# The attention output of blocks 2 to 14 turned by transposing transfers, and the first sums of the down weights later

## The chip, the cores and the metric

The kernel runs on one core of a Trainium2 chip. The metric is the device time of one execution in microseconds (us), the median of several runs. The profile names the engines PE (TensorE, matrix products; PEld loads the stationary operand), DVE (VectorE), ACT (ScalarE), POOL (GpSimd) and SP (SyncE, which here issues nearly all transfers).

## The reference

One transformer block on x of 2048 rows and 640 columns in float32: layer norm, attention of 32 heads of 20 columns in which a row sees itself and the 255 rows ahead of it, the product with wo added to x, and a gated feed-forward layer with 1536 hidden columns.

```
def _A_ref(x, wqkv, wo):          # H = 32, Dh = 20, W = 256
    q, k, v = ...                 # (x @ wqkv) by heads
    scores = einsum("bhqd,bhkd->bhqk", q, k) * Dh ** -0.5
    mask = (idx[:, None] - idx[None, :] >= 0) & (idx[:, None] - idx[None, :] < W)
    p = softmax(where(mask, scores, -1e9))
    o = einsum("bhqk,bhkd->bhqd", p, v)
    return o.transpose(0, 2, 1, 3).reshape(B, S, D) @ wo
def _B_ref(x, w_gate, w_up, w_down):
    return (gelu(x @ w_gate) * (x @ w_up)) @ w_down
h  = x + _A_ref(layernorm(x), wqkv, wo)
h2 = h + _B_ref(layernorm(h), w_gate, w_up, w_down)
```

## The kernel before, in words

**Tiling.** The 2048 rows are 16 blocks of 128 rows (j = 0 to 15). A dense product of float32 precision is made of three products of halves: each operand is split into a float16 "hi" (a cast) and a float16 "lo" (the value less hi), and hi·hi, hi·lo and lo·hi are summed in PSUM. `parts` (line 556) lists the three, `products` (568) issues them, and `quarters` (560) cuts a 128-wide stationary operand into four 32-wide ones where the planner takes PE to be in the state in which the p·v products leave it. PE contracts over partitions, so an operand whose columns are contracted must be turned first: 128 rows by 640 columns become five squares of 128 by 128.

**Stages.** In the first some 640 us attention and the first parts of the feed-forward layer run interleaved; behind that the feed-forward layer runs alone, with a scheme that saves products by sums of operands (`Quad`, `down7`). For a block of attention: x is loaded and normalised (`x_lane`, line 706), turned, multiplied into q and k, which go to DRAM and come back by heads (`stack`, line 801: six loads each into qT and kT on SP); maxima and scores are made for pairs of heads in PSUM (`ra`, `rb`), the exponentials by ACT (`pt`), the mask by POOL, p·v on PE (`pv`). ACT copies four steps of p·v into oT, and `normalise` (1081), once for each half of the heads, turns oT by four PE transposes into PSUM (`tp`), from which DVE takes the reciprocal of the row sums (`rec`) and writes the quotient into `o32` (printed `o` by the profile). Behind the second half `o_transpose` (1102) turns o32: five PE transposes in two groups (four and one) into PSUM, each followed by ACT's cast to oh and DVE's subtraction to ol (`transpose_part`, 543). Then the block's number goes into `woq`, and `wo_block` (1120) makes its products with wo (its halves are w3h and w3l); `wo_out` adds x on DVE and writes h on SP.

**Two ways to turn.** `transpose_part` is the one on PE. `turned` (526) is the other: ACT casts the whole block to hi, DVE subtracts to lo, both in an SBUF buffer that is read as two float16 halves, and SP issues a transposing transfer (DMA_TRANSPOSE) of 128 by 640 for each. x's blocks from 4 on use it, with the buffer `xp`, one copy of it, into xh and xl; h of the feed-forward layer uses it too. A counter lets one such turn of x begin at a time.

**What sets the order.** Each engine runs its instructions in the order in which the program issues them. That order is found when the program is built: the class Clock keeps an estimated clock for each engine, every piece of work is a generator (a "lane") that yields what its next instruction needs, and the loop at the end issues the next instruction of the first lane that could start, in a fixed order of lanes (work on finished PSUM results first, then turns, outputs, side work, then attention or dense products). `normalise` and `o_transpose` may be held back up to an estimated 2 us so that they fall between other kinds of products. SP's instructions stand in one order too; one that must wait for its data holds those behind it. All instructions are recorded by one helper, so all have line 199; the tiles tell them apart.

**Sums of down weights.** `seven_weights` (1398) prepares, for a later stage of the feed-forward layer, four sums of the halves of the down weights: POOL subtracts (ts<-w10l), DVE adds (ts<-w10h), POOL, DVE. Its first step waits in the planner until a count of finished "quads" has reached FT = 4 and two weights are used up.

Of the kernel before, what the change touches and what calls it, by code (L numbers as in the profile page):

```python
# [11 lines left out]
F32 = mybir.dt.float32  # L12
F16 = mybir.dt.float16
# [8 lines left out]
S, D, H, DH, F = 2048, 640, 32, 20, 1536  # L22
P = 128
NB = S // P
KC = D // P
# [5 lines left out]
FT = 4  # L31
# [18 lines left out]
def _pow2(e):  # L50
    return float(2.0 ** e)
# [202 lines left out]
def block_kernel(ctx: ExitStack, tc: tile.TileContext, x, wqkv, wo, wg, wu, wd, out):  # L254
# [12 lines left out]
    opened, pos = Counter(), Counter()  # L267
# [11 lines left out]
    def ps_tp(dt=F32):  # L279
        return bank("tp", dt)  # L280

    def done(name):
        opened[name] -= 1
# [10 lines left out]
    NR = 4  # L294
# [17 lines left out]
    def need(*reads, slots=(), when=None, eng="tensor"):  # L312

        def f():
            if when and not when() or any(opened[n] >= banks[n] for n in slots):
                return INF
            return max([nc.ready(reads, eng)]
                       + [nc.slot(psums[n], n, banks[n]) for n in slots])
        return f

    def pe(*reads, slots=(), when=None):
        return ("tensor",), need(*reads, slots=slots, when=when)

    def on(eng, *reads, when=None, after=None):
        f = need(*reads, when=when, eng=eng)
        if after is not None:
            return (eng,), lambda: max(f(), nc.others(after, eng))
        return (eng,), f
# [4 lines left out]
    def soon(eng, *reads):  # L333
        return Soon((eng,)), need(*reads, eng=eng)
# [143 lines left out]
    W = {}  # L478
# [47 lines left out]
    def turned(src, lane, to, dst=None, when=None, two=None):  # L526

        key = "xparts" if dst else "parts"
        yield on("scalar", src, when=lambda: not opened[key] and (not when or when()))
        opened[key] += 1  # L530
        two = (two if dst else lnbuf[2]).bitcast(F16)
        hi, lo = two[:, :D], two[:, D:]
        nc.scalar.copy(hi, src)
        yield on("vector", hi)
        nc.vector.tensor_tensor(lo, src, hi, op=ALU.subtract)
        if dst:
            to = dst()
        for o, i in zip(to, (hi, lo)):
            yield ("sync",), need(i, eng="sync")
            nc.sync.dma_start_transpose(o, i)  # L540
        opened[key] -= 1
# [99 lines left out]
    maxq, tps, scoreq, valq, woq = [], [], deque(), deque(), deque()  # L641
# [45 lines left out]
    class Block:  # L687
# [3 lines left out]
        h, turned, normed, full = None, False, False, False  # L691
# [7 lines left out]
    B = [Block() for _ in range(NB)]  # L699
# [3 lines left out]
        b.c, b.cols = C[j // 2], slice((j % 2) * P, (j % 2) * P + P)  # L703
    at = lambda n, shape, dt, bufs=2: nc.tile(att, shape, dt, n, bufs)

    def x_lane(blocks, lane):

        for j in blocks:
            c = C[j // 2]
            if j > 1:  # L710
                yield on("vector", when=lambda: W["k" if j < NR else "v"].scaled)
            if j >= NR and j + 1 < NB:
                yield ("sync",), lambda: max(0.0, nc.slot(att, "xt", 2))
                load_x(j + 1)

            def dst():
                if j < 2:
                    return x32[:, :, B[j].cols], None
                return xparts(j)

            yield from layernorm(B[j].x, lane, None, None, dst,
                                 lambda: j < 6 or c.x or C[j // 2 - 3].used == 4,
                                 lambda: B[j].x, tp="rb" if j in (1, 3) else "tp",
                                 dma=j >= NR and at("xp", [P, D], F32, 1))
            if j < 2:
                B[j].full = True
                tasks.append(x_cast(j))
            else:
                B[j].ready = True

    def xparts(j):
        c = C[j // 2]
        if c.x is None:
            c.x = tuple(nc.tile(wq, [P, KC, CW], F16, n, 3) for n in ("xh", "xl"))
        return tuple(t[:, :, B[j].cols] for t in c.x)

    def x_cast(j):
        src = x32[:, :, B[j].cols]
        yield on("scalar", src, when=lambda: W["k"].scaled)
        hi, lo = xparts(j)  # L740
        nc.scalar.copy(hi, src)
        yield on("gpsimd", hi)
        nc.gpsimd.tensor_tensor(lo, src, hi, op=ALU.subtract)
        B[j].ready = True

    def load_x(j):
        if 0 < j < NR:
            t = at("pt", [P, 4, 3, P], F32, 3).rearrange("p a b c -> p (a b c)")
            B[j].x = t[:, 0:D]
        else:  # L750
            B[j].x = at("xt", [P, D], F32)
        nc.sync.dma_start(B[j].x, x[j * P:(j + 1) * P, :])
# [328 lines left out]
    def normalise(j, half, oT):  # L1081
        b = B[j]
        yield pe(oT, slots=["tp"], when=lambda: j == 0 or half or B[j - 1].normal)
        if half == 0:
            b.o32 = at("o32", [P, H, DH], F32, 1)
        t = ps_tp()
        OR = 3 * 32 + DH + 1
        for u4 in range(4):
            nc.tensor.transpose(t[:, u4 * P:u4 * P + OR], oT[:OR, u4, :], ident[:OR, :OR])
        pos["normal"] += 1  # L1090
        tv = t.rearrange("p (h e) -> p h e", e=32)
        rec = at("rec", [P, 16], F32)
        yield soon("vector", t)
        nc.vector.reciprocal(rec, tv[:, :, DH])
        yield soon("vector", rec)
        nc.vector.tensor_tensor(b.o32[:, 16 * half:16 * half + 16, :], tv[:, :, 0:DH],
                                rec[:, :, None].to_broadcast([P, 16, DH]), op=ALU.mult)
        done("tp")
        if half:
            tps.append(o_transpose(j))  # L1100

    def o_transpose(j):
        b = B[j]
        src = b.o32.rearrange("p h d -> p (h d)")
        for part, (c0, c1) in enumerate(((0, 4), (4, 5))):
            yield pe(src[:, c0 * P:c1 * P], slots=["tp"],
                     when=lambda: part or j < 2 or B[j - 2].wrote)
            if part == 0:
                b.oh, b.ol = at("oh", [P, KC, P], F16), at("ol", [P, KC, P], F16)
            yield from transpose_part(src, b.oh, b.ol, c0, c1)  # L1110
        b.normal = True
        woq.append(j)
# [284 lines left out]

    def seven_weights():

        yield on("gpsimd", when=lambda: pos["quads"] >= FT and W["u", 1].spent  # L1400
                 and W["u", 2].spent)
        t = nc.tile(ffp, [P, KC, 512], F32, "ts0").rearrange("p c n -> p (c n)").bitcast(F16)
        n = FT * N2
        t1, t2, t3, t4 = ST["t"] = [t[:, i * n:(i + 1) * n].rearrange("p (f n) -> p f n", n=N2)
                                    for i in range(4)]
        ul = [W["u", g].hl[1].rearrange("p c f -> p (c f)") for g in (1, 2)]
        ST["z"] = [ul[0].bitcast(F32)[:, i * N2:(i + 1) * N2] for i in range(4)]
        ST["s"] = [ul[1][:, i * FT * P:(i + 1) * FT * P].rearrange("p (f n) -> p f n", n=P)
                   for i in range(4)]
        for g, (c, fg) in enumerate(SEVEN):  # L1410
            dh, dl = W["d", fg].hl
            d1, d2, e1, e2 = dl[:, :, :N2], dl[:, :, N2:], dh[:, :, :N2], dh[:, :, N2:]
            free = lambda n: lambda: pos["visits"] >= 8 * (g - 1) + n
            yield on("gpsimd", dl, when=free(6))
            nc.gpsimd.tensor_tensor(t1, d2, d1, op=ALU.subtract)
            yield on("vector", t1, dh, when=free(6))
            nc.vector.scalar_tensor_tensor(t2, e2, _pow2(-TE), t1, op0=ALU.mult, op1=ALU.subtract)
            pos["t", g] = 2
            yield on("gpsimd", t2, when=free(7))
            nc.gpsimd.tensor_tensor(t3, t2, d1, op=ALU.subtract)  # L1420
            pos["t", g] = 3
            yield on("vector", t2, when=free(8))
            nc.vector.scalar_tensor_tensor(t4, t2, -_pow2(TE), e1, op0=ALU.mult, op1=ALU.add)
            pos["t", g] = 4
# [457 lines left out]
    for i, n in enumerate("qkv"):  # L1882
        W[n].load(rooms[n])
        W[n].room(wq)
        if i:
            load_x(i + 1)
    load_x(NR)
    lanes = [x_lane([0], "x"), x_lane([1], "xb"), x_lane([2], "xc"), x_lane([3], "xd"),
             x_lane(range(NR, NB), "x"),
             split_lane(), *(scale_lane([i], str(i)) for i in range(NW)),  # L1890
             scale_lane(range(NW, len(weights)), "0"), load_lane(), ones_lane(), big_lane(),
# [95 lines left out]
```

## Time and profile before

| | before |
|---|---|
| median of 3 runs | 995.48 us (994.24 to 996.4) |
| profiled execution | 996.4 us |
| its span on the core | 994.7 us |
| granted PE clock, mean | 0.996 |
| DMA traffic | 113.01 MB, 114 GB/s in the mean |

The span is the time between the first and the last instruction on the core; 1.7 us of the profiled execution lie around it. An engine's busy time is the union of its instructions; PE's products overlap, so a group's duration is more than it holds PE. "x -> y" in the profile's rows is written y<-x: the tile written, then those read. A mark like [0.50 <-ACT oh] at a row's end is the idle time before it on its engine and what ended that.

### The profile page before, as it was taken

How to read it: one execution, taken by the hardware profiler on the slowest of the kernel's cores; microseconds unless marked ns; L12 is line 12 of the kernel's file. 1: busy time of each engine (PE TensorE's matmuls, PEld its weight loads, DVE VectorE, ACT ScalarE, POOL GpSimd, SP SyncE). 2: the span in 40 equal slices, each digit the busy share in tenths (PEclk: the TensorE clock that was granted, in tenths of full speed). 3: DMA queues.
4: the chain of work that ended last, by engine and by line, in shares of the span. 5: the costliest groups of instructions: out<-in, count | busy, mean ns of one | idle time of the engine just before them, and what ended most of it. 6: DMA issues, size and time to landing. Idle time of an engine off the chain costs nothing.

```text
span 994.7 us, 35811 instructions
## 1 busy us (share of the span) xinstructions
PE 977.8 (98%) x15326; PEld 747.6 (75%) x15326; DVE 787.4 (79%) x2252; ACT 485.7 (49%) x862; POOL 342.0 (34%) x498
## 2 busy tenths in 40 slices
PE   8998999999999999999999999999999999999998
PEld 7875777777877777777766754688788888888886
DVE  7878998887876767777688798877976887788784
ACT  5615657675555555555577535343323333443431
POOL 7003335463434333344346311344303223233320
PEclk9999999999999999999999999999999999999999
DMA  8667565752522433222305543324354442223211
GB/s 314 126 124 181 148 171 161 172 140 76 112 81 70 109 87 81 72 69 70 124 31 124 113 136 104 109 80 132 119 175 106 148 144 81 80 80 107 81 54 53
DMA packets 130047, 113.01 MB, mean 114 GB/s; under 512 B 85216, under 2 KB 103392, under 8 KB 129888
## 3 DMA queue, kind: packets, MB, share of 16 engines
q1 hardware_dynamic: 117792, 99.97, 36.6%
q10 hardware_dynamic: 12096, 10.75, 3.4%
q8 instruction: 120, 1.97, 0.8%
q14 instruction: 39, 0.32, 0.1%
HBM read 73.73 MB, written 28.84 MB: 103 GB/s over the span
## 4 chain that ended last, share of the span: by engine, by line
PE 86%; DVE 8%; ACT 3%; DMA 2%; issue 1%; POOL 0%; SPq 0%; ACTq 0%; DVEq 0%
PE mm L199 40%; PE rb L199 12%; PE ra L199 12%; PE pv L199 11%; PE tp L199 9%; DVE junk L199 1%; DVE ts L199 1%; DVE am L199 1%; ACT pt L199 1%; DVE ht L199 1%; DMA wst<-in_wu_dram 0%; DVE w1l L199 0%; DMA wst<-in_wd_dram 0%; DMA pt<-in_x_dram 0%; DVE xt L199 0%
## 5 line engine op out<-in xcount | busy, mean ns | idle before, releaser
L199 POOL TENSOR_SCALAR_AFFINE_SELECT pt<-pt 128x512 f32<-128x512 f32 x352 | 176.5, 517 | 270.0 <-ACT pt L199 252.6
L199 DVE CUSTOM_DVE_ANT_0 junk<-rb,band 128x320 bf16<-128x320 f32 x232 | 113.4, 489 | 36.1 <-PE rb L199 31.1
L199 ACT ACTIVATE pt<-ra,esc 128x640 f32<-128x640 f32 (+2 forms) x132 | 100.6, 769 | 78.0 <-PE ra L199 68.8
L199 ACT ACTIVATE pt<-rb,esc 128x640 f32<-128x640 f32 (+2 forms) x124 | 94.3, 768 | 81.9 <-PE rb L199 75.4
L199 DVE CUSTOM_DVE_ANT_0 junk<-ra,band 128x320 bf16<-128x320 f32 x216 | 105.7, 489 | 33.9 <-PE ra L199 28.9
L199 PE MATMUL pv<-pt,v 128*21 128x128 f32 x2880 | 103.0, 275 | 0.3 <-ACT oT L199 0.2
L199 PEld LDWEIGHTS <-ah 128*128 128x128 f16 (+1 forms) x660 | 63.5, 98 | 23.2 <-issue 1.0
L199 PEld LDWEIGHTS <-ws 128*128 128x128 f16 x720 | 70.8, 98 | 12.9 <-issue 2.6
L199 PEld LDWEIGHTS <-qT 60*64 60x64 f16 x1280 | 29.7, 104 | 62.3 <-issue 51.3
L199 PEld LDWEIGHTS pv<-pt,v 128*21 128x21 f32 x2880 | 69.2, 100 | 9.6 <-issue 1.1
L199 PEld LDWEIGHTS <-kT 62*64 62x64 f16 x2880 | 64.4, 106 | 9.3 <-issue 5.3
L199 PEld LDWEIGHTS <-gu 128*128 128x128 f16 (+1 forms) x700 | 51.7, 98 | 26.1 <-issue 0.4
L199 DVE SCALAR_TENSOR_TENSOR ht<-mm,ffk,ht 128x320 f32<-128x320 f32 x86 | 46.9, 545 | 15.4 <-PE mm L199 14.2
L199 PE MATMUL mm<-xh,w1h 128*32 128x256 f16 (+1 forms) x344 | 55.9, 273 | 1.4 <-DVE qks L199 1.4
L199 PE MATMUL mm<-xl,w1h 128*32 128x256 f16 (+1 forms) x362 | 56.0, 273 | 0.0
L199 PE MATMUL mm<-xh,w1l 128*32 128x256 f16 (+1 forms) x356 | 55.9, 273 | 0.0
L199 ACT CAST ah<-gel 128x512 f16<-128x512 f32 x48 | 29.7, 619 | 47.8 <-DVE gel L199 47.7
L199 DVE TENSOR_TENSOR al<-gel,ah 128x512 f16<-128x512 f32 x48 | 42.3, 882 | 13.1 <-ACT ah L199 12.1
L199 ACT ACTIVATE gel<-gel,ffk 128x512 f32<-128x512 f32 x36 | 26.0, 723 | 50.2 <-DVE gel L199 50.1
L199 PE MATMUL mm<-w3h,oh 128*32 128x320 f16 (+1 forms) x364 | 49.7, 299 | 0.6 <-DVE ht L199 0.6
L199 PE MATMUL mm<-w3h,ol 128*32 128x320 f16 (+1 forms) x355 | 49.6, 299 | 0.0
L199 PE MATMUL mm<-w3l,oh 128*32 128x320 f16 (+1 forms) x355 | 49.6, 299 | 0.0
(354 smaller groups left out, 2670.2 us busy)
## 6 DMA issues: line engine op xcount, KB each, us to landing
ws<-wsums SPq DMA_DIRECT2D x24, 640.0 KB
qk<-qks ACTq DMA_DIRECT2D x32, 256.0 KB
wsums<-ws SPq DMA_DIRECT2D x12, 640.0 KB
qT<-qk SPq DMA_DIRECT2D x72, 80.0 KB
kT<-qk SPq DMA_DIRECT2D x72, 80.0 KB
ht<-in_x_dram SPq DMA_DIRECT2D x16, 320.0 KB
h_dram<-ht SPq DMA_DIRECT2D x16, 320.0 KB
ht<-h_dram SPq DMA_DIRECT2D x16, 320.0 KB
```

Of the source, the lines that this page charges most:

```text
L199: r = real(*args, **kw)
```

## The change

Three edits. First, the buffer xp is taken once, ahead of `x_lane`, in place of a request in each block. Second, for blocks 2 to 14 `o_transpose` no longer turns o32 on PE: it calls `turned` with its own counter for o and x together, the same buffer xp, and fresh tiles oh and ol as the targets; it may begin once block j - 2 has written h. The block counts as normalised when its two transfers are issued, and the first half of `normalise` of the next block waits for that in the planner. Blocks 0, 1 and 15 are turned as before. Third, `seven_weights` begins at 2·FT = 8 finished quads in place of 4.

```
--- before.py
+++ after.py
@@ -703,6 +703,8 @@
+    xp = at("xp", [P, D], F32, 1)
+
     def x_lane(blocks, lane):
@@ -721,7 +723,7 @@
-                                 dma=j >= NR and at("xp", [P, D], F32, 1))
+                                 dma=j >= NR and xp)
@@ -1082,6 +1084,7 @@
         b = B[j]
         yield pe(oT, slots=["tp"], when=lambda: j == 0 or half or B[j - 1].normal)
         if half == 0:
+            yield pe(when=lambda: j == 0 or B[j - 1].normal)
             b.o32 = at("o32", [P, H, DH], F32, 1)
@@ -1102,6 +1105,15 @@
     def o_transpose(j):
         b = B[j]
         src = b.o32.rearrange("p h d -> p (h d)")
+        if 1 < j < NB - 1:
+            def dst():
+                b.oh, b.ol = at("oh", [P, KC, P], F16), at("ol", [P, KC, P], F16)
+                return b.oh, b.ol
+
+            yield from turned(src, "o", None, dst, lambda: B[j - 2].wrote, xp)
+            b.normal = True
+            woq.append(j)
+            return
         for part, (c0, c1) in enumerate(((0, 4), (4, 5))):
@@ -1397,7 +1409,7 @@
     def seven_weights():
 
-        yield on("gpsimd", when=lambda: pos["quads"] >= FT and W["u", 1].spent
+        yield on("gpsimd", when=lambda: pos["quads"] >= 2 * FT and W["u", 1].spent
                  and W["u", 2].spent)
```

The function it calls, as it stands in both:

```
def turned(src, lane, to, dst=None, when=None, two=None):
    key = "xparts" if dst else "parts"
    yield on("scalar", src, when=lambda: not opened[key] and (not when or when()))
    opened[key] += 1
    two = (two if dst else lnbuf[2]).bitcast(F16)
    hi, lo = two[:, :D], two[:, D:]
    nc.scalar.copy(hi, src)
    yield on("vector", hi)
    nc.vector.tensor_tensor(lo, src, hi, op=ALU.subtract)
    if dst:
        to = dst()
    for o, i in zip(to, (hi, lo)):
        yield ("sync",), need(i, eng="sync")
        nc.sync.dma_start_transpose(o, i)
    opened[key] -= 1
```

What the change moves, at three places. On PE at block 12, where the first four transposes of o32 stood between a score group (rb<-qT,kT) and dense products of v (w2h, w2l with x's halves):

```order
L199 LDWEIGHTS kT
L199 MATMUL rb<-qT,kT 64x64
L199 MATMUL tp<-ident,o_12167 128x128 x4
L199 LDWEIGHTS xl
L199 MATMUL mm<-w2h,xl 128x320
L199 LDWEIGHTS xh
L199 MATMUL mm<-w2h,xh 128x320
```

and where, in the changed kernel, the first product with wo now stands (w3h with oh), the rows around it:

```order
L199 LDWEIGHTS xh
L199 MATMUL mm<-w2l,xh 128x320
L199 LDWEIGHTS xl
L199 MATMUL mm<-w2h,xl 128x320
L199 LDWEIGHTS oh
L199 MATMUL mm<-w3h,oh 128x320
L199 LDWEIGHTS qT
L199 MATMUL rb<-kT,qT 64x320
```

The transposes are gone from between the scores; the first product with oh stands four pairs of maxima and scores behind the last transpose of oT, where it stood six behind it before, and one pair of maxima now separates it from the next product with wo.

On SP around block 8, before: the loads of q and k of one pair of blocks (six for each block), the write of h and the load of the next row of x for the residual.

```order
L199 DMA h_dram<-ht 128x640
L199 DMA ht<-in_x_dram 128x640
L199 DMA qT<-qk_8008 20x16x128 x6
L199 DMA kT<-qk_8793 20x16x128 x6
L199 DMA h_dram<-ht 128x640
```

And in the changed kernel, the same loads under other buffer numbers:

```order
L199 DMA h_dram<-ht 128x640
L199 DMA ht<-in_x_dram 128x640
L199 DMA qT<-qk_8266 20x16x128 x6
L199 DMA_TRANSPOSE oh<-xp 128x5x128
L199 DMA_TRANSPOSE ol<-xp 128x5x128
L199 DMA kT<-qk_8937 20x16x128 x6
L199 DMA h_dram<-ht 128x640
```

The two transposing transfers of o stand behind the six loads of qT and ahead of those of kT.

On DVE in the last stage, the first sums of the down weights (ts<-w10h) among the work on results of quads (gel, rs, ht) and on sums of h (wst), as a piece of the difference with its marks:

```order
 L199 TENSOR_TENSOR al<-gel,ah 128x512
 L199 SCALAR_TENSOR_TENSOR ht<-mm,ffk,ht 128x320
-L199 SCALAR_TENSOR_TENSOR ts_16367<-w10h,ts_16367 128x1280
-L199 TENSOR_TENSOR gel<-tp,rs 128x256
-L199 SCALAR_TENSOR_TENSOR ts_16367<-ts_16367,w10h 128x1280
+L199 TENSOR_TENSOR gel<-tp,rs 128x256
 L199 TENSOR_TENSOR rs<-rb,rs 128x256
 L199 TENSOR_TENSOR gel<-rb,gelt 128x256
```

The two sums come back some 27 rows later, on either side of a product's result (ht) and the product of gate and up (gel). POOL's rows keep their order there:

```order
L199 TENSOR_TENSOR ws<-w5h,ws 128x640
L199 TENSOR_TENSOR ts_16605<-w10l 128x1280
L199 TENSOR_TENSOR ts_16605<-ts_16605,w10l 128x1280
L199 TENSOR_TENSOR lyh<-lveh,mhalf 128x1
L199 TENSOR_TENSOR lyi<-lvei,mhalf 128x1
```

These five rows stand the same way in both kernels, under another buffer number.

## The prediction

> **What bounds the kernel now.** I read the page first, its totals and the chain that ended last:
>
> ```profile
> span 994.7 us, 35811 instructions
> PE 977.8 (98%) x15326; PEld 747.6 (75%) x15326; DVE 787.4 (79%) x2252; ACT 485.7 (49%) x862; POOL 342.0 (34%) x498
> PE 86%; DVE 8%; ACT 3%; DMA 2%; issue 1%; POOL 0%; SPq 0%; ACTq 0%; DVEq 0%
> PE mm L199 40%; PE rb L199 12%; PE ra L199 12%; PE pv L199 11%; PE tp L199 9%; DVE junk L199 1%; DVE ts L199 1%; DVE am L199 1%; ACT pt L199 1%; DVE ht L199 1%; DMA wst<-in_wu_dram 0%; DVE w1l L199 0%; DMA wst<-in_wd_dram 0%; DMA pt<-in_x_dram 0%; DVE xt L199 0%
> ```
>
> TensorE (PE) is busy for 98% of the span and holds 86% of the chain; ScalarE (ACT) is busy for half of it. A share over the whole span mixes stages, so I cut it. The columns are the window, its length, the busy time of PE, PEld, DVE, ACT and POOL with counts, the granted PE clock, the share of the DMA engines and their GB/s:
>
> ```profile
> 100.00:330.00 230.00, 227.45 (x5247) 175.08 (x5244) 191.99 (x702) 140.57 (x227) 101.68 (x181) 1.00 0.51 125
> 330.00:570.00 240.00, 239.55 (x5764) 175.61 (x5763) 178.75 (x606) 144.47 (x225) 100.16 (x197) 1.00 0.34 86
> 640.00:995.00 355.00, 348.71 (x2938) 288.14 (x2937) 276.53 (x515) 123.05 (x271) 98.79 (x63) 0.99 0.32 103
> ```
>
> The attention of blocks 2 to 14 lies in the first two windows. PE is idle there for 2.6 and 0.5 us, DVE for 38 and 61, ACT for 89 and 96. So a product taken from PE there shortens the run by what it took, as long as nothing arrives late in its place. The clock is at 1.00, so fewer products bring no faster ones.
>
> **What the first part removes.** The timeline of PE around block 12 shows the instructions that go, each row one group (start, length, tile written <- tiles read, count):
>
> ```profile
> 475.05 0.62 PE L199 MATMUL tp<-ident,oT 117*128 117x117 f32 x4
> 475.51 0.30 PE L199 MATMUL mm<-w2l,xh 128*128 128x320 f16 x1
> 478.56 0.66 PE L199 MATMUL tp<-ident,o 128*128 128x128 f32 x4
> 479.05 0.30 PE L199 MATMUL mm<-w2h,xl 128*128 128x320 f16 x1
> 482.36 0.33 PE L199 MATMUL tp<-ident,o 128*128 128x128 f32 x1
> 482.53 0.30 PE L199 MATMUL mm<-w2h,xl 128*128 128x320 f16 x1
> 486.39 0.30 PE L199 MATMUL mm<-w3h,oh 128*128 128x320 f16 x1
> ```
>
> Products are pipelined, so I price by the step from one start to the next: the four transposes hold PE for 479.05 - 478.56 = 0.49 us, the fifth for 482.53 - 482.36 = 0.17 us. That is 0.66 us a block, and for the 13 blocks 2 to 14 **8.6 us**. The groups of PE give the count and a second price:
>
> ```profile
> L199 PE MATMUL mm<-xh,w1h 128*128 128x256 f16 x152 | 41.5, 273 | 1.4 <-DVE qks L199 1.4
> L199 PE MATMUL tp<-ident,o 128*128 128x128 f32 x80 | 15.4, 290 | 0.0
> L199 PE MATMUL mm<-xh,w1h 128*32 128x256 f16 x192 | 14.4, 273 | 0.0
> ```
>
> 80 transposes are 16 blocks of five; 65 go. At 15.4 us busy for 80, 65 would be 12.5 us; those durations overlap, so it is the upper end and 8.6 the value.
>
> **What it adds on PE.** In the order of the changed kernel 44 more dense products stand in a place where they are cut into four 32-wide ones. Four such cost 14.4/48 = 0.300 us of busy time, one whole product 41.5/152 = 0.273: 27 ns each, 1.2 us for 44, the upper end, since the rows of both kinds overlap. I take it whole. Nine filling products fewer at the start bring nothing, because they stand where PE waits anyway. So PE's own work falls by 8.6 - 1.2 = **7.4 us**.
>
> **What it adds elsewhere.** DVE's, then ACT's part of the turn of block 12:
>
> ```profile
> 475.98 0.25 DVE L199 RECIPROCAL rec<-tp 128x16 f32<-128x16 f32 x1
> 476.27 0.49 DVE L199 TENSOR_TENSOR o<-tp,rec 128x320 f32<-128x320 f32 x1
> 480.07 0.69 DVE L199 TENSOR_TENSOR ol<-tp,oh 128x512 f16<-128x512 f32 x1 [0.50 <-ACT oh L199]
> 483.55 0.29 DVE L199 TENSOR_TENSOR ol<-tp,oh 128x128 f16<-128x128 f32 x1 [0.18 <-ACT oh L199]
> ```
>
> ```profile
> 479.46 0.58 ACT L199 CAST oh<-tp 128x512 f16<-128x512 f32 x1
> 483.26 0.26 ACT L199 CAST oh<-tp 128x128 f16<-128x128 f32 x1
> ```
>
> The same work for x's turn is in the view of the tile xp (shortest, median and longest ns):
>
> ```profile
> L199 ACT CAST xp<-xt x12: 710/725/736, 47.1 to 326.2; 128x640 f16<-128x640 f32 x12
> L199 DVE TENSOR_TENSOR xp<-xt,xp x12: 817/820/1247, 48.0 to 327.0; 128x640 f16<-128x640 f32 x12
> ```
>
> ACT goes from 0.58 + 0.26 = 0.84 to 0.73 us a block, DVE from 0.98 to 0.82 (1.25 at worst): a little less on two engines that have 39% (ACT) and 17% (DVE) or more to spare in those windows. That is worth nothing on the path. The price is latency: the halves must now be cast, subtracted and carried by two transfers before PE reads them. I bound it by x's own turns. The quickest one behind the first 100 us, and the slowest:
>
> ```profile
> 258.98 0.72 ACT L199 CAST xp<-xt 128x640 f16<-128x640 f32 x1
> 261.44 1.89 SPq L199 DMA_TRANSPOSE xl<-xp  x1
> ```
>
> ```profile
> 152.26 0.73 ACT L199 CAST xp<-xt 128x640 f16<-128x640 f32 x1
> 156.90 6.61 SPq L199 DMA_DIRECT2D kT<-qk  x3
> 164.95 1.21 SPq L199 DMA_TRANSPOSE xl<-xp  x1
> ```
>
> From the cast's start to the issue of the second transfer: 2.5 us, and 12.7 us where SyncE (SP) stood 6.6 us in loads of kT placed ahead of it. The landing shows where the first user waits for such a transfer, with h in the last stage:
>
> ```profile
> 758.65 1.82 SPq L199 DMA_TRANSPOSE h1h<-wsl  x1
> 761.70 0.73 ACT L199 CAST wsl<-wsl 128x640 f16<-128x640 f32 x1 [3.07 <-DMA h1h<-wsl]
> 761.42 1.20 SPq L199 DMA_TRANSPOSE h1l<-wsl  x1
> 764.09 0.82 DVE L199 TENSOR_TENSOR wsl<-wsl 128x640 f16<-128x640 f32 x1 [0.89 <-DMA h1l<-wsl]
> ```
>
> 761.70 - 758.65 = 3.05 us and 764.09 - 761.42 = 2.67 us from issue to landing. The chain of a block then is: from the last transpose of oT (about 475.4) to the end of o's second half (476.27 + 0.49) 1.35 us, cast to second issue 2.5, landing 2.7 to 3.05: 6.5 to 6.9 us, and with one ACT and one DVE instruction ahead about 8.2. I take **7.4**.
>
> What the chain has to fit into is the way on PE from the last transpose of oT to the first product with oh. Before, at block 12, it was 486.39 - 475.4 = 11.0 us with three rounds (a round is two pairs of maxima and scores, one step of p·v and the dense products between), 3.7 us a round. In the new order two rounds stand there, 7.3 us and a few dense products (7.9), and the product with ol one pair later. Blocks 2, 3 and 8 have two and a half rounds (9.0 to 9.4), the other nine 10.2 to 21.7; the 13 blocks average 12.1. So the undisturbed chain fits everywhere, barely at block 12, and a turn held like the slow one of x does not: 10.2 us later than the quick one, less 12.1 - 7.4 = 4.7 of room, is 5.5 us of PE standing still, and everything queued behind that product on PE (maxima, scores, p·v) stands with it. One in twelve of x's turns was held so; with 13 turns I expect one, and as much as none: the value is between 0 and 5.5, about **2.6 us**. The ends are 0 (no hold) and 17 (two holds at blocks with 9.2 us of room: 2 x (10.2 - 1.7)).
>
> SP itself issues 26 more transfers of about 1.2 us, 31 us in the 470 us of both windows; loads behind them come later by 2.4 us a block, and q and k rows are loaded well ahead of their use. Moving xp to one allocation for both users adds a wait only where x's turn and o's turn meet; they meet in blocks 2 to 8, and the key that lets one turn begin at a time puts o's behind x's by at most one quick turn, 2.5 + 2.7 us. The new wait in the first half's normalisation stands in the planner and not on the chip; it puts those transposes a little later in PE's order.
>
> The Trainium skill speaks against this edit: "VectorE: DVE Perf Modes", section "The three transpose paths" and the rules behind it, prices a 128x128 transpose at 390 ns on TensorE and 1309 ns by transfer, and keeps the transfer for destinations that can't be PSUM. By an estimate from that page a half of five squares would land after 6.5 us, both after 13.1, the chain would be some 15 us, and the run about 50 us longer; the landings above, 3.05 and 2.67 us for five squares, disagree, so I leave it no chance of its own.
>
> **The third part.** The later first sums of the down weights aim at a place where PE stands still:
>
> ```profile
> PE tp L199 <- ACT rr L199: 2.2, 1, 2.2
> ```
>
> ```profile
> 702.88 2.60 POOL L199 TENSOR_TENSOR ts<-w10l 128x1280 f16<-128x1280 f16 x1
> ```
>
> ```profile
> L199 DVE TENSOR_SCALAR wsl<-wsl,lmvi,lyi x6: 603/612/2853, 541.8 to 781.1; 128x640 f32<-128x640 f32 x6
> ```
>
> ```profile
> 702.97 2.85 DVE L199 TENSOR_SCALAR wsl<-wsl,lmvi,lyi 128x640 f32<-128x640 f32 x1
> ```
>
> DVE's instruction, 612 ns in the median of its six, starts 0.09 us after POOL's first sum and ends 0.3 us after it; what DVE and ACT have to do with PE's results comes late, and PE waits 2.2 us. But in POOL's new order that sum stands where it stood, behind the same sum of weights (ws<-w5h,ws) and with nothing of its own to wait for; only DVE's two sums (ts<-w10h) move, some 27 rows on. So the collision stays: **nothing**, with 2.2 us of gain (it goes) and 2.2 us of loss (a second one of its size) as ends. The Trainium skill, "SBUF — State Buffer", section "SBUF: two separate sides", calls the pair of ports that VectorE shares with GpSimd an exclusive lock, held for a whole instruction; the two rows agree, and by it the gap goes only if POOL's sum is moved.
>
> **The sum.** -7.4 + 2.6 + 0 = -4.8 us. The profiled run took 996.4 us, its span and 1.7 us around it; that is 0.9 above the median of 995.48. So 991.6 against the profiled run, **990.7** against the median. A measurement of this kernel can tell about 0.2%, 2 us, from no change.
>
> **Rivals.** *Given back*: one turn held fully at a block with little room (10.2 - 1.7 = 8.5 us) against 7.4 of gain: 996.6, or, with the average room of 4.7 us, 993.6. For it speaks that new transfers of blocks 4, 6 and 8 stand right behind six loads of qT, and those of 5, 7, 9 and 11 among loads of kT; against it that these loads mostly belong to a group that has begun. *Slower*: SP stands still in front of the transposing transfers at two of the blocks 2, 3, 8 and 12, because the loads ahead wait for rows of q and k that are not yet written. Price 2 x 8.5 = 17 us, less 7.4: 995.5 + 9.6 = 1005.1. It decides from 9.4 us of new waits on. *More gain*: no hold, the quarters at nothing and the collision gone: -8.6 - 2.2 = -10.8, 984.7; with the first two alone 986.9. That the first part doesn't do what it says is ruled out by the order; that the third doesn't is my forecast.
>
> **How the numbers follow.** Forecast (988 to 993.5) 0.62, more gain (below 988) 0.08, given back (993.5 to 997.5) 0.18, slower (above) 0.12. The range leaves out half of the gain's case, the upper end of the second and the slow case, about 0.2: 986.5 to 996.5. Faster by over 0.2% is the first two, 0.70; within 0.18; slower 0.12.
>
> **What would show it.** tp<-ident,o 15 times instead of 80, PE's busy time lower by 7 to 9 us; 13 transfers each into oh and ol; in the waits of PE a new line of dense products on the transfer of oh or ol, 0 to 6 us in all, at few blocks; the end of attention earlier by about what PE saved less that line; the 2.2 us on ACT rr still there. Wrong would be: waits on oh or ol above 7 us, a landing well over 3 us, or q and k loads that now arrive after PE asks for them.

## The result, and the profile after

| | before | after |
|---|---|---|
| median | 995.42 us (994.24 to 996.78, 6 runs) | 1006.41 us (1004.38 to 1011.55, 6 runs) |
| ratio to before | | 1.0122, 95% interval 1.0102 to 1.0141 |
| profiled execution, span | 996.4, 994.7 us | 1004.54, 1002.8 us |

The change makes the kernel 1.2% slower; the forecast was 0.5% faster. The page after, its totals and its chain:

```profile
span 1002.8 us, 35973 instructions
PE 974.0 (97%) x15384; PEld 741.3 (74%) x15384; DVE 788.2 (79%) x2239; ACT 486.2 (48%) x849; POOL 341.3 (34%) x498
PE 81%; DVE 10%; ACT 3%; issue 3%; DMA 1%; POOL 1%; ACTq 0%; SPq 0%; DVEq 0%; POOLq 0%
PE mm L199 40%; PE rb L199 11%; PE ra L199 11%; PE pv L199 11%; PE tp L199 8%; DVE junk L199 4%; ACT pt L199 1%; DVE ws L199 1%; DVE m L199 0%; DVE w1l L199 0%; ACTq L199 0%; DVE wsl L199 0%; DMA xh<-xp 0%; DMA ol<-xp 0%; DVE ht L199 0%
```

PE is busy for 3.8 us less (974.0 for 977.8), where the forecast had 7 to 9, and yet the span is 8.1 us longer. A part of the saving is hidden: the mean granted PE clock fell from 0.996 to 0.992, by estimate some 4 us of the span, and a product with oh lasts up to 474 ns, where its median is 299. PE's idle time, the span less its busy time, rose from 16.9 to 28.8 us. The windows (length, busy time of PE, PEld, DVE, ACT and POOL, granted PE clock, DMA share, GB/s) show where:

```profile
100.00:330.00 230.00, 218.48 (x5026) 165.21 (x5028) 183.19 (x662) 132.54 (x210) 94.30 (x170) 0.97 0.57 126
330.00:570.00 240.00, 238.21 (x5886) 172.54 (x5877) 182.87 (x621) 146.11 (x218) 105.33 (x205) 1.00 0.43 98
640.00:995.00 355.00, 351.69 (x2972) 290.54 (x2970) 285.19 (x526) 123.69 (x273) 98.61 (x64) 1.00 0.33 106
```

Between 100 and 330 us PE now stands idle for 11.5 us where it stood 2.6, and its clock is 0.97 in place of 1.00. What it waits for, by the list of PE's waits (sum, times, longest):

```profile
PE rb L199 <- ACT pt L199: 5.3, 2, 4.7
PE ra L199 <- DVE mxs L199: 4.4, 5, 2.1
PE tp L199 <- ACT rr L199: 2.7, 2, 2.2
PE ra L199 <- ACT pt L199: 2.6, 5, 0.7
PE pv L199 <- DVE pv L199: 2.5, 1, 2.5
```

The same list of before names no wait on ACT pt, and on DVE mxs these two lines:

```profile
PE ra L199 <- DVE mxs L199: 2.0, 1, 2.0
PE rb L199 <- DVE mxs L199: 1.1, 3, 0.6
```

So the waits that grew are on exponentials (ACT pt) and maxima (DVE mxs). A wait of PE for a transfer of oh or ol, which the forecast looked for, isn't among them.

The longest wait can be followed. PE first, then ACT, then SP around 151 us of the changed kernel (start, length; in brackets the idle time before and what ended it):

```profile
151.20 0.33 PE L199 MATMUL ra<-kT,qT 60*64 60x320 f16 x4
156.27 0.48 PE L199 MATMUL rb<-qT,kT 62*64 62x128 f16 x12 [4.75 <-ACT pt L199]
```

```profile
149.27 0.24 ACT L199 CAST h0h<-tp 128x128 f16<-128x128 f32 x1
154.80 0.72 ACT L199 CAST xp<-xt 128x640 f16<-128x640 f32 x1 [5.29 <-DMA xh<-xp]
155.43 0.79 ACT L199 ACTIVATE pt<-rb,esc 128x640 f32<-128x640 f32 x1
```

```profile
142.89 7.56 SPq L199 DMA_DIRECT2D kT<-qk  x6
150.55 1.24 SPq L199 DMA_TRANSPOSE xh<-xp  x1
151.90 2.30 SPq L199 DMA_TRANSPOSE xl<-xp  x1
```

SP stands in loads of kT for 7.6 us, so the transfer of xh is issued at 150.55, 12.3 us after its cast began at 138.23. ACT has come to the next block's cast into xp, which must not overwrite what that transfer still reads. It waits 5.29 us, and the exponential behind it, which waits for nothing of the kind, waits with it; so does PE. Both turns are of x: the first cast of o comes later, at 179 us. In the kernel before, the same turn (cast at 137.05) had its transfers ahead of most of these loads:

```profile
138.46 2.27 SPq L199 DMA_TRANSPOSE xh<-xp  x1
142.47 1.21 SPq L199 DMA_TRANSPOSE xl<-xp  x1
145.40 10.90 SPq L199 DMA_DIRECT2D kT<-qk  x7
```

### The profile page after: what moved, and what is told of

Same layout as the page of the kernel before. It is cut to its first block, busy times and chain, and to the rows that moved or that the text cites. A ratio compares the mean times of both kernels' runs of the same rounds, so it can differ in the third digit from the quotient of the medians.

```text
span 1002.8 us, 35973 instructions
## 1 busy us (share of the span) xinstructions
PE 974.0 (97%) x15384; PEld 741.3 (74%) x15384; DVE 788.2 (79%) x2239; ACT 486.2 (48%) x849; POOL 341.3 (34%) x498
## 4 chain that ended last, share of the span: by engine, by line
PE 81%; DVE 10%; ACT 3%; issue 3%; DMA 1%; POOL 1%; ACTq 0%; SPq 0%; DVEq 0%; POOLq 0%
PE mm L199 40%; PE rb L199 11%; PE ra L199 11%; PE pv L199 11%; PE tp L199 8%; DVE junk L199 4%; ACT pt L199 1%; DVE ws L199 1%; DVE m L199 0%; DVE w1l L199 0%; ACTq L199 0%; DVE wsl L199 0%; DMA xh<-xp 0%; DMA ol<-xp 0%; DVE ht L199 0%
## 5 line engine op out<-in xcount | busy, mean ns | idle before, releaser
L199 DVE CUSTOM_DVE_ANT_0 junk<-rb,band 128x320 bf16<-128x320 f32 x224 | 109.5, 489 | 35.9 <-PE rb L199 31.0
L199 DVE CUSTOM_DVE_ANT_0 junk<-ra,band 128x320 bf16<-128x320 f32 x224 | 109.5, 489 | 35.3 <-PE ra L199 30.3
L199 ACT ACTIVATE pt<-ra,esc 128x640 f32<-128x640 f32 (+2 forms) x131 | 98.1, 757 | 79.2 <-PE ra L199 68.1
L199 PEld LDWEIGHTS <-ah 128*128 128x128 f16 x648 | 63.4, 98 | 23.4 <-issue 1.1
L199 PE MATMUL mm<-xl,w1h 128*128 128x256 f16 (+1 forms) x344 | 56.1, 273 | 0.0
```

The source lines that it names most:

```text
L199: r = real(*args, **kw)
```

## The experiments

Two theories stood at the start. **A**: turns that meet in the one buffer xp make casts (ACT) and subtractions (DVE) stand, with exponentials and maxima behind them. **B**: the planner found another order, and the order of before is a good one among many.

To compare orders I priced PE's work from the traces: the median step between the starts of two products, for each pair of kinds in the trace of before, summed over a kernel's own order. What is left up to PE's last product is waiting and slower clock. A saving of work and a loss by waits are then told apart. The two columns are my estimate; no view of the profile has them, their level depends on how the kinds are drawn, and only their differences are used:

| run | ratio to before, 95% interval | PE work, us | rest, us |
|---|---|---|---|
| before | 1 | 962.4 | 25.9 |
| after | 1.0122 (1.0102 to 1.0141) | 954.6 | 41.5 |
| xp once | 1.0131 (1.0113 to 1.0148) | 962.3 | 37.4 |
| blocks 10 to 14 only | 1.0003 (0.9993 to 1.0014) | 959.8 | 27.1 |
| after, cast when xp is free | 1.0094 (1.0073 to 1.0115) | 955.1 | 41.3 |
| after, sums as before | 1.0105 (1.0079 to 1.0132) | 954.6 | 41.1 |
| xp once, marked | 1.0001 (0.9988 to 1.0013) | 962.4 | 27.9 |
| after, marked | 1.0060 (1.0041 to 1.0080) | 956.4 | 39.7 |
| xp once, a cast later | 1.0081 (1.0064 to 1.0099) | 962.0 | 34.3 |
| before, 0.185 | 1.0072 (1.0051 to 1.0093) | 960.9 | 31.9 |
| own buffers, blocks 5 to 12 | 1.0034 (1.0021 to 1.0047) | 957.4 | 32.7 |
| own buffers, blocks 4 to 11 | 1.0014 (1.0000 to 1.0028) | 957.6 | 34.7 |
| before, 0.21 | 1.0050 (1.0028 to 1.0072) | 963.5 | 28.0 |
| before, sums later | 1.0010 (1.0000 to 1.0019) | 962.4 (same order) | not taken |

The median of before was 994.6 to 996.3 us in these sets of runs; the two columns on the right are of one profiled execution each. The pages' own totals go the same way: PE's idle time is 16.9 us before, 28.8 after, 26.6 with xp once, 17.2 with xp once, marked, and 28.1 with the change marked.

### xp once, nothing else

```
+    xp = at("xp", [P, D], F32, 1)
-                                 dma=j >= NR and at("xp", [P, D], F32, 1))
+                                 dma=j >= NR and xp)
```

> The kernel before with xp taken once and nothing else; o32 is turned on PE as before. The planner then finds another order. Theory A (casts and subtractions stand on ACT and DVE because the one buffer xp is still being read by held transfers, and the exponentials and maxima stand behind them): no o turns use xp, so within 2 us of 995.4. Theory B (any new order costs, because the order of before is a good one among many): 4 us slower or more, 999 to 1003, with the PE stall of some 5 us near 150 us of the changed kernel.

Measured: 1008.52 us against 995.35, all of the loss and 2 us more, without one turn of o. The stall is the one of the changed kernel, by the list of PE's waits and ACT's row:

```profile
PE rb L199 <- ACT pt L199: 4.6, 1, 4.6
```

```profile
154.42 0.72 ACT L199 CAST xp<-xt 128x640 f16<-128x640 f32 x1 [5.14 <-DMA xh<-xp]
```

So A as put (turns of o) is not the cause of this part; the edit that looked like tidying is.

### Transfers for blocks 10 to 14 only

```
+        if 9 < j < NB - 1:
+            ...
+            yield from turned(src, "o", None, dst, lambda: B[j - 2].wrote, at("xp", [P, D], F32, 1))
```

> The kernel before, with only blocks 10 to 14 turned by transfers, when x's turns are over; the order is that of before up to block 10. Theory A: no turn meets another, so the gain of PE shows: 5 x 0.66 = 3.3 us, 992. Theory B: the order behind block 10 is new, 0 to 3 us slower than before, 995 to 998.

Measured: 995.64 against 995.35 us. PE's work is 2.6 us less and no turn meets another (x's last cast is at 326 us, o's first at 418), yet nothing is gained that the spread would show: in the part with the new order there are two waits that before doesn't have, by PE's list from 400 to 640 us:

```profile
PE pv L199 <- ACT oT L199: 1.2, 1, 1.2
PE mm L199 <- issue: 1.1, 1, 1.1
```

The first is a copy of oT late on ACT; what the second, "issue", stands for the trace doesn't show.

### The changed kernel with casts planned when xp is free

```
-        yield on("scalar", src, when=lambda: not opened[key] and (not when or when()))
+        yield on("scalar", src, when=lambda: not opened[key] and (not when or when()),
+                 after=two if dst else None)
```

> The changed kernel, with one thing more: the planner lets a turn's cast start only when by its own clock xp is free again. Theory A: ACT stands less for xp, 5 us or more off the changed kernel, 996 to 1001. Theory B: one more new order, 1000 to 1010 without a trend.

Measured: 1005.29 us, 1 us less than the 1006.4 of the change, which the spread of both covers: a miss for A. PE still waits 4.45 us at 151 us. The planner's clock took the buffer for free: it doesn't know that SP stands 7 us in the loads ahead of the transfer. In this order PE does wait for ol, 2.9 us in two places.

### The third edit, taken out of the change and put alone into before

```
-        yield on("gpsimd", when=lambda: pos["quads"] >= 2 * FT and W["u", 1].spent
+        yield on("gpsimd", when=lambda: pos["quads"] >= FT and W["u", 1].spent
```

> The changed kernel with the third edit undone (first sums of the down weights at 4 finished quads). Both theories: within 2 us of the changed kernel's 1006.4, since POOL's rows stand in the same order; if the later sums help, up to 1.5 us slower than the changed kernel.

> The kernel before with the third edit alone: the first sums of the down weights at 8 finished quads. PE's and POOL's orders are those of before; DVE's first two sums stand some 27 rows later. If the sums of POOL alone make the stall at 704 us, it stays at 2.2 us and the time is 996 within 1.5 us. If DVE's sums had a part in it, 2 to 3 us faster.

Measured: 1005.48 us without it in the changed kernel, and 995.97 against 994.61 with it alone (ratio 1.0010, interval 1.0000 to 1.0019). The interval leaves room for 0.2% of loss and for no gain. POOL's sum and PE's wait in the changed kernel:

```profile
711.82 2.60 POOL L199 TENSOR_TENSOR ts<-w10l 128x1280 f16<-128x1280 f16 x1
```

```profile
715.90 0.71 PE L199 MATMUL tp<-h1l,ws 128*128 128x256 f16 x5 [2.20 <-ACT rr L199]
```

The same 2.2 us as before, and with the edit alone they are there too, by PE's list of that kernel:

```profile
PE tp L199 <- ACT rr L199: 2.2, 1, 2.2
```

### xp once, with the mark of a fresh request

A request for a tile tells the planner that the whole buffer is in use until its last use ends. A buffer kept is recorded by its halves: the hi cast is planned to wait for the hi transfer alone. This kernel keeps the buffer but restores the mark, in the planner only:

```
+    def again():
+        key = xp.tensor.name if hasattr(xp, "tensor") else xp.name
+        nc.wr[key] = [((0, 128, 0, 1 << 30), "ring", nc.quiet(key))]
+        return xp
-                                 dma=j >= NR and xp)
+                                 dma=j >= NR and again())
```

> The kernel before with xp taken once, as in the first of these runs, but with the planner told at each block's turn that the whole buffer is in use until its last use ends, which is what a fresh request tells it. Every engine's order is then that of before; only the waits of the finer-grained buffer on the chip differ. If the order is what costs: 995.4 within 2 us. If the waits of the one buffer cost (the cast waits for the hi transfer alone, the subtraction for the lo transfer): most of the 13 us of the first run, 1003 to 1009.

Measured: 996.19 against 996.15 us. The rows of every engine stand as in before, and the time is that of before, though on the chip a cast now waits for the hi transfer alone, as in the first run (before, ACT once stood 2.7 us for xl; here it doesn't). So the 13 us of the first run are the order, not the buffer.

### The changed kernel with the same mark

> The changed kernel with the same mark at each turn of x and o. The order is that of before up to block 2's turn of o, so the stall near 151 us (4.9 us, with what follows it some 8 us) is not planned. If the loss is that order: 996 to 999, the PE work saved (7.8 us) against the waits that the turns of o bring behind 180 us (some 8 us in the changed kernel). If turns of o are what costs: 1004 or more.

The edit is again() for xp in both calls. Measured: 1002.25 us, 4 us better than the change and 6 worse than before: between the two expectations. The stall at 151 us isn't there: between 140 and 170 us no step of PE is more than 1 us over its usual length, as in before. In its place is one that turns of o do make. ACT, SP and PE near 280 us:

```profile
275.87 0.72 ACT L199 CAST xp<-o 128x640 f16<-128x640 f32 x1 [3.76 <-DVE mxs L199]
286.08 0.72 ACT L199 CAST xp<-xt 128x640 f16<-128x640 f32 x1 [7.62 <-DMA oh<-xp]
```

```profile
276.42 4.72 SPq L199 DMA_DIRECT2D kT<-qk  x5
281.25 1.26 SPq L199 DMA_TRANSPOSE oh<-xp  x1
```

```profile
287.55 0.48 PE L199 MATMUL ra<-kT,qT 60*64 60x128 f16 x8 [3.57 <-ACT pt L199]
```

o's cast at 275.87, its transfer held by five loads of kT until 281.25, x's next cast standing on ACT for 7.62 us behind it: A's mechanism, with 3.6 us of PE. In the changed kernel it shows near 216 us on DVE, whose subtraction must not overwrite the lo half that x's transfer still reads:

```profile
211.10 1.22 SPq L199 DMA_TRANSPOSE xl<-xp  x1
```

```profile
216.63 0.83 DVE L199 TENSOR_TENSOR xp<-o,xp 128x640 f16<-128x640 f32 x1 [3.86 <-ACT qks L199]
217.38 0.48 DVE L199 CUSTOM_DVE_ANT_0 junk<-ra,band 128x320 bf16<-128x320 f32 x1
```

```profile
218.46 0.34 PE L199 MATMUL ra<-qT,kT 62*64 62x128 f16 x12 [2.07 <-DVE mxs L199]
```

The row names ACT's qks, but the subtraction needs only o's cast, done at 213.07, and the transfer. It was the transfer: in the trace its semaphore gets the last update at 216.54, 5.4 us after the issue, and DVE's wait for that semaphore ends at 216.57.

### A cast moved behind an exponential

To the kernel with xp once, block 9's cast is planned only when ACT's clock is 8 us past the issue of block 8's transfers; then an exponential and the copy of oT stand ahead of it on ACT.

```
+                                 lambda: (j < 6 or c.x or C[j // 2 - 3].used == 4) and (
+                                     j != 9 or nc.t["scalar"] > turn[0] + 8),
+                turn[0] = nc.t["sync"]
```

> The first of these runs (xp once) with block 9's cast planned later, so that an exponential and the copy of oT stand ahead of it on ACT. If the cast standing on ACT is what holds the exponentials: the PE wait of 4.8 us near 151 us falls under 1 us and the time by 3 us or more, 1005 or less. If it was the loads of k and q as such that came late: the wait stays at 4 to 5 us.

Measured: 1004.30 us for 1008.52 (in another set of runs; ratios 1.0081 and 1.0131). ACT's and PE's rows:

```profile
154.17 0.72 ACT L199 CAST xp<-xt 128x640 f16<-128x640 f32 x1 [1.49 <-DMA xh<-xp]
162.77 0.72 ACT L199 ACTIVATE gu<-wsl,sw 128x512 f16<-128x512 f32 x1 [3.46 <-DMA wsl<-in_wg_dram]
```

```profile
165.04 0.48 PE L199 MATMUL rb<-kT,qT 60*64 60x320 f16 x4 [3.78 <-ACT pt L199]
```

The cast now waits 1.49 us, and the wait of PE at 151 us is gone, as expected. But 10 us later ACT stands 3.46 us for a slice of weights that SP loads late, and PE loses 3.8 us there. Which engine stands is the order's choice; what makes it stand, here as at 151 us, is a transfer that SP issues late.

### Two other orders, with nothing of the change

```
-    LAT = 0.18
+    LAT = 0.185
```

> The kernel before with one constant of the planner changed from 0.18 to 0.185 (the estimated delay between engines); the instructions are the same but for fillers and quarters, the order is another. If the order of before is a lucky one: 4 us slower or more, 1000 to 1008. If an order costs only through turns of the one buffer xp: 994 to 998.

```
-    AHEAD, APART = 0.2, 1.0
+    AHEAD, APART = 0.21, 1.0
```

> The kernel before with another constant of the planner changed, from 0.2 to 0.21 (how far ahead PE is filled); no edit of the change is in it. If the order of before is a lucky one: 3 us slower or more, 999 to 1008. If the first such run was the exception: 994 to 998.

Measured: 1003.32 and 999.96 us, against 996.15 and 996.32. A constant changed by 3 or 5% costs 0.7 and 0.5%. Where the first one lost most, DVE and PE:

```profile
164.63 0.61 DVE L199 TENSOR_SCALAR ht<-ht,lmvh,lyh 128x640 f32<-128x640 f32 x1 [5.45 <-DMA h_dram<-ht]
```

```profile
165.30 1.11 PE L199 MATMUL tp<-ident,ht 128*128 128x128 f32 x4 [5.22 <-DVE ht L199]
```

The same pattern in another buffer than xp: DVE stands 5.45 us for a buffer that a transfer of h, issued on SP at 160.12, still reads.

### o's turns in buffers of their own

The kernel before, with o of blocks 5 to 12 (then 4 to 11) turned through the buffers of the weight slices, which are free by then, under a counter of their own. xp is left as it was, and the order is that of before up to the first such turn.

```
+        if 5 <= j <= 12:
+            ...
+            yield from turned(src, "o", None, dst, lambda: B[j - 2].wrote,
+                              nc.tile(stage, [P, D], F32, "wsl", SLICES))
```

> The kernel before, with blocks 5 to 12 of o turned by transfers through buffers of their own (those of the weight slices, free by then), so that no turn of o meets one of x; the order is that of before up to block 5's turn near 260 us. If turns that meet are what o's transfers cost: no cast on ACT waits for a transfer of oh or ol, PE's work falls by 8 x 0.66 = 5.3 us, 991 to 993. If a new order costs by itself: 996 to 1000, with new PE waits at other places.

> The same with blocks 4 to 11, so the order is new from block 4's turn near 230 us on, when x's turns are denser. If meetings are the cost: as the run before, 991 to 993. If a new order costs by itself: another number, 994 to 1002.

Measured: 999.70 and 997.88 against 996.32 us. PE's work falls by 5.0 and 4.8 us; no cast stands for o's transfers; and neither is faster, as a cost of the new order had it and a cost of meetings alone had not. In the first the forecast's own mechanism appears, at block 8, on SP and PE:

```profile
334.80 6.47 SPq L199 DMA_DIRECT2D kT<-qk  x2
341.37 1.22 SPq L199 DMA_TRANSPOSE oh<-wsl  x1
```

```profile
345.30 0.31 PE L199 MATMUL mm<-w3h,oh 128*128 128x320 f16 x1 [2.01 <-DMA oh<-wsl]
```

Two loads of kT hold SP for 6.5 us, oh is issued at 341.37, and PE waits 2.0 us for it. The second has a wait of 2.4 us and a mean clock of 0.91 between 40 and 60 us, ahead of its first changed row, where before has neither; its profiled execution was the slowest of its 12 (1000.64 us), so a part of its rest is chance of one execution.

## Why the prediction was wrong

**What PE saves was about right.** Forecast 7.4 us less work; by the priced order it is 7.8. PE's busy time with the stretches of clock 0.50 counted half, another estimate from the two traces, gives 6.4. The transposes of o32 fell from 80 to 15:

```profile
L199 PE MATMUL tp<-ident,o 128*128 128x128 f32 x15 | 2.8, 282 | 0.0
```

**The step that failed** is the one that priced the first edit: "Moving xp to one allocation for both users adds a wait only where x's turn and o's turn meet". It was taken for a matter of waits on the chip. On the chip it costs nothing (ratio 1.0001 with the order held), but in the planner it changes what a turn waits for, and with that the order of all engines from the first such turn on. That alone takes 13 us (ratio 1.0131). The order was used to price PE's own work and the distance from oT to the products with oh; what the new order does to ACT, DVE and SP was not priced at all. Rest of 25.9 us before, 41.5 after: by this estimate 15.6 us of new waits and slower clock against 7.8 us saved, in the two profiled executions, which differ by 8.1 us; the medians differ by 11.

**The term of new waits, 2.6 us, was looked for in the wrong place.** It stood for PE waiting for oh or ol. In the changed kernel that wait isn't in PE's list: from the cast to the issue of the second transfer o's 13 turns took 2.2 to 6.8 us, none near the 12.7 of the held one. What was late was the next cast or subtraction into xp, on engines that the forecast had with 39% and 17% to spare: spare time doesn't help an instruction that stands in front of the others.

**Two readings fell short.** The landing, 2.7 to 3.05 us, was read in the last stage. In the attention stage the instructions that waited for such a transfer started 4.25 us (150.55 to 154.80), 5.5 us (211.10 to 216.63), 4.8 us (281.25 to 286.08) and 3.9 us (341.37 to 345.30) after its issue; a landing well over 3 us was one of the forecast's own signs of being wrong. And of x's twelve turns before, two were held and not one: ahead of 100 us one took 34.9 us, from its cast at 54.57 to its second transfer at 89.50. In the changed kernel neither makes PE wait for oh or ol; the longer landing is a part of the waits for xp.

**The slower rival** had the time (1005.1 for 1006.4) and the root (SP standing in loads of q and k ahead of transposing transfers), but not the way: it went over PE's wait for oh, and the transfers held were x's as much as o's. That the number fits is luck.

**The third edit** was right: POOL's sum stays, and the 2.2 us with it.

How the 11 us divide between order and meetings is not settled. The order of xp once costs 13 us without any turn of o; with before's order kept up to block 2, the change costs 6 us, in which the meeting near 280 us is seen; and the change has both, with 7.8 us of work less. No run has the order of one with the turns of the other. Whether the 26 more transfers also make others land later (the DMA share of the second window went from 0.34 to 0.43) was not tested. Nor was a version found that beats before.

## What to carry to other kernels

Where a program's order is found by a planner, an edit is two edits: what it does, and the new order; a neutral change of a constant (here two, 0.5 and 0.7%) hints at how much the second is worth, and an edit worth less than that can't be judged by one build. Before pricing an edit that only moves a request or a buffer, ask what the planner takes from it; restoring the planner's view while keeping the edit tells the two apart. And for each wait that a change can bring, price the instructions queued behind the waiting one on its own engine, not only the one that needs the data.

## What the runs showed of the hardware

A stall of PE can cost more than its length. The changed kernel's windows around the stall at 151 us, and behind it (columns as above, the granted clock third from the end):

```profile
151.00:156.20 5.20, 0.53 (x12) 0.13 (x5) 0.50 (x1) 1.40 (x3) 0.00 (x0) 0.86 0.96 124
156.20:161.30 5.10, 5.03 (x44) 3.27 (x43) 4.22 (x13) 3.85 (x7) 3.77 (x5) 0.50 0.88 225
161.30:166.00 4.70, 4.70 (x122) 3.88 (x118) 3.75 (x17) 2.94 (x5) 2.53 (x6) 0.98 0.67 191
```

For 5.1 us behind it the granted clock is 0.50. If products go by the granted clock, that is some 2.5 us more lost: by this estimate a stall of 4.75 us took about 7. The changed kernel behind the wait of 2.07 us at 216 us, and behind that of 2.20 us at 713 us:

```profile
220.00:226.00 6.00, 5.67 (x95) 3.47 (x98) 4.44 (x15) 2.47 (x4) 3.00 (x6) 0.50 0.75 145
713.50:720.00 6.50, 4.30 (x40) 3.68 (x38) 5.14 (x9) 3.14 (x7) 0.93 (x1) 1.00 0.41 128
```

The shorter wait was followed by some 6 us at half clock, the longer one by none. In the kernel before, the same wait of 2.20 us, at 704 us, was followed by half clock too:

```profile
708.00:710.00 2.00, 2.00 (x11) 1.44 (x10) 2.00 (x4) 0.05 (x1) 0.00 (x0) 0.50 0.36 69
```

So the length of the wait alone doesn't decide it. The Trainium skill, "TensorE: Matmul & The Clock Gate", section "Part 1: The HAM clock gate", has the clock at half after an idle window of about 3.4 us and back after as much of steady work. Here the clock was at half for some 6.8 us around the stall at 151 us (the mean of 0.86 over 5.2 us makes 1.5 of them, inside the stall), and the waits of 2.07 and 2.20 us, shorter than that window, were each followed by half clock once; there the measurement decides.
